# Fewer idle products at the start, x tiles 0 and 1 on ScalarE's queue, wv ahead of x tiles 4 to 7, and another order behind 72 fixed operations: an adaLN block on one Trainium2 core

## The chip, the core and the metric

The kernel runs on one core of a Trainium2 chip. The metric is the device time of one execution in microseconds, the median over several runs. A core has TensorE (PE in the profile; its weight loads have a row of their own, PEld), VectorE (DVE), ScalarE (ACT), GpSimd (POOL) and SyncE (SP), and 16 DMA engines that all queues share. Each engine takes its instructions strictly in the order of its own list, so an instruction that waits holds up all behind it.

## What is computed

The input x has 2048 rows of 512 values, in bfloat16. Cut to what matters:

```python
mod = (silu(c) @ w_mod).reshape(1, 6, 1, 512)
sa, ca, ga, sb, cb, gb = mod[:, 0], ..., mod[:, 5]
h = layernorm(x) * (1 + ca) + sa
x = x + ga * A(h)       # attention: 32 heads of 16; row s sees rows s, s-2, ..., s-14; then @ wo
h = layernorm(x) * (1 + cb) + sb
x = x + gb * B(h)       # (silu(h @ w1) * (h @ w3)) @ w2, hidden width 1792
```

c is one row of 512 values, w_mod is 512 x 3072, wqkv is 512 x 1536, wo 512 x 512, w1 and w3 512 x 1792, w2 1792 x 512.

## The kernel before, in words

The rows of x are 16 tiles T of 128 rows. Nothing is ordered by loops: `_build` makes a list of 1197 operations (`Program.op`), each with its engine, a function that emits its instructions, and the values that it reads and writes. Two long lists written into the file, `ORDER` and `SLOTS`, then say in which order the operations are put onto their engines and which buffer (or PSUM bank) each value takes. `Program.place` deals `ORDER` out to the five engines' lists, and `Program.synchronize` adds a semaphore wait wherever an operation needs another engine's result or a buffer that is still in use. So `ORDER` fixes each engine's instruction list, SyncE's DMA list among them; a DMA is issued by SyncE unless it is built with another `eng`. The costs given to the operations (among them `WMOD`, `PACKET` and `MM`) are of use only to the search that made the lists; no instruction depends on them.

The steps that the text below speaks of, with the profile's line numbers:

- *The modulation.* c is loaded by a DMA of ScalarE's queue, goes through a tanh (L456, after a load of ScalarE's function table) and two VectorE operations (L458, L460), is turned into columns by a TensorE transpose (L462) and copied to `csz` (L464). The first third of w_mod (shift and scale of the first layer norm) comes in four pieces `wms0_0` to `wms0_3` of 256 KB, one DMA each. `modulation(0)` multiplies each piece as it comes (L480, 32 products of 8 columns in all, eight to a piece), and L491 copies the result to `modc`.
- *Idle products.* `warm(n)` puts n products of `ones` with `ones` on TensorE (L502, 512 columns each), whose result nobody reads. `WARMS` says how many stand ahead of the first, second, third and fourth piece, and how many after the last.
- *The first layer norm.* Per tile VectorE takes the statistics (L542, L543), GpSimd the power -0.5 (L547, L549), VectorE normalizes (L554), TensorE transposes (L614), and ScalarE (L622) or VectorE (L629) evict with shift and scale into `h`, which needs `modc`. Tiles are grouped `LN1` = [0, 1], [2, 3], [4..7], [8..11], [12..15]; the last group is transposed by DMA.
- *Projections.* q and k by L666 with evictions at L674 and L675, v by L685 with eviction at L695 and a store to a scratch in DRAM. Group [0, 1] is multiplied piece by piece as the four parts of `h` are there; the other groups wait for the whole of `h`.
- *Attention*, for two tiles at a time: VectorE multiplies q with eight shifted k (L716), TensorE sums over each head (L725, 32 small tiled products), a softmax runs on VectorE and ScalarE, 4 DMAs per tile fetch shifted v from the scratch (`vsh`), VectorE weighs them (L800), TensorE sums (L809, 8 tiled products in four column strips), ScalarE evicts (L815), a DMA transposes, TensorE multiplies with wo (L833) and VectorE adds to x (L837).
- *The gated feed-forward*, for the groups `FFN`: w1 and w3 products (L849, 256 or 512 columns), then w2 products (L892, and L880 for the last two tiles), and the sum with x (L908) goes out. w1, w3 and w2 come in four column groups each, so a product on columns `fi` needs the group's DMA alone (`w1_0` holds the column blocks fi 0 to 3, and so on).

All loads but c are DMAs of SyncE. Its list begins x0, x1, the four pieces, wk, x2 and x3, wq, x4 to x7, wv, x8 to x11, x12 to x15.

Of the kernel before, what the change touches and what calls it, by code (L numbers as in the profile page):

```python
# [267 lines left out]
WMOD = 120  # L268
WARMS = (8, 3, 3, 4, 2)
# [9 lines left out]
def _build(p, A_x, A_wqkv, A_wo, B_w1, B_w3, B_w2, c, w_mod, out):  # L279
# [4 lines left out]
    x_view = x2d.rearrange("(t p) d -> p t d", p=P)  # L284
# [4 lines left out]
    x_sb = sb([P, NT, D], bf, "x")  # L289
# [120 lines left out]
    vx = [Val(f"x{T}") for T in range(NT)]  # L410
# [7 lines left out]
    for T in range(2):  # L418
        p.dma(x_sb[:, T, :], x_view[:, T, :], ("load", 1), (128, 1024), w=[vx[T]])
# [580 lines left out]
]  # L1000
SLOTS = [
# [47 lines left out]
```

## Time and profile before

| | |
|---|---|
| median of 3 runs | 242.54 us (242.08, 242.72, 242.54) |
| the profiled execution's own time | 242.59 us |
| its span, first to last instruction | 240.6 us |
| granted TensorE clock in the profile | 1.00 |
| TensorE busy | 232.7 us, 97% of the span |
| VectorE / ScalarE busy | 168.3 us (70%) / 157.9 us (66%) |
| DMA | 38.33 MB, 159 GB/s over the span |
| idle products L502 | 20 in the program, 19 in the records, 534 ns mean |

The profiled execution is 2.0 us longer than its span and 0.05 us over the median. TensorE's busy time counts each product from its start to its modelled end, and products overlap, so a long busy bar does not mean that products start as fast as they can. How fast they start is read from the times between starts: 0.43 us for a product of 512 columns early on, 0.216 us later, and half of that for 256 columns. A few records of products are missing.

### The profile page before, as it was taken

The page shows a single profiled execution, that of the slowest core. Times are in us where ns is not written, and L with a number is a line of the kernel's source. Part 1 is how long each engine was busy: PE and PEld are TensorE (multiplying, and loading weights), DVE is VectorE, ACT ScalarE, POOL GpSimd, SP SyncE. Part 2 cuts the span into 40 slices and gives each one's busy share as a digit, 9 for nine tenths or more (in the row PEclk, how much of TensorE's full clock was granted, in tenths as well). Part 3 has the DMA queues.
Part 4 walks back from the last instruction along what each step waited for, and adds up shares of the span by engine and source line. Part 5 has one row for each costly group of instructions (what it writes and reads, how often), then busy time and mean ns, then how long its engine had stood idle before and what let it go on. Part 6 is the DMA issues. An engine that isn't in the chain of part 4 may idle for free.

```text
span 240.6 us, 4592 instructions
## 1 busy us (share of the span) xinstructions
PE 232.7 (97%) x1794; PEld 136.3 (57%) x1820; DVE 168.3 (70%) x287; ACT 157.9 (66%) x329; POOL 21.1 (9%) x54
## 2 busy tenths in 40 slices
PE   7989999999999999999999999999999999999995
PEld 2557644545577867664444444444474447576774
DVE  4489999999999999999999658335453224152352
ACT  2169687988999888768858988746754583422310
POOL 4254110000001000130000110001000100000000
DMA  6997999699499959696875963454302000301011
GB/s 191 354 321 226 284 227 248 188 289 346 131 243 270 280 163 226 183 315 101 236 184 166 204 196 75 100 152 45 89 15 52 3 0 3 85 24 65 3 44 45
DMA packets 44125, 38.33 MB, mean 159 GB/s; under 512 B 19512, under 2 KB 34888, under 8 KB 44104
## 3 DMA queue, kind: packets, MB, share of 16 engines
q1 hardware_dynamic: 44096, 38.04, 59.5%
q8 instruction: 14, 0.23, 0.4%
q14 instruction: 7, 0.06, 0.1%
q10 hardware_dynamic: 8, 0.00, 0.0%
HBM read 29.62 MB, written 4.21 MB: 141 GB/s over the span
## 4 chain that ended last, share of the span: by engine, by line
PE 79%; DMA 7%; ACT 5%; DVE 3%; SPq 2%; issue 2%; POOL 1%
PE pall L849 32%; PE pall L892 14%; PE pall L666 10%; PE pall L833 5%; PE pall L685 4%; DMA sb_w<-in_B_w_dram 4%; PE pall L809 3%; PE pall L725 3%; PE pall L502 3%; PE pall L880 3%; SPq L124 2%; DMA sb_h<-sb_xn 2%; DMA out_dram<-sb_o 2%; PE pall L614 1%; ACT sb_h L622 1%
## 5 line engine op out<-in xcount | busy, mean ns | idle before, releaser
L849 PE MATMUL pall<-sb_h,sb_w 128*128 128x256 bf16 (+1 forms) x666 | 102.5, 308 | 1.1 <-ACT sb_hh L859 0.4
L849 PEld LDWEIGHTS pall<-sb_h,sb_w 128*128 128x128 bf16 x672 | 64.7, 98 | 37.3 <-ACT sb_hh L859 1.5
L855 ACT ACTIVATE sb_sg<-pall 128x256 bf16<-128x256 f32 (+1 forms) x84 | 36.5, 457 | 33.3 <-PE pall L849 29.4
L892 PE MATMUL pall<-sb_w,sb_hh 128*128 128x512 bf16 x189 | 43.4, 379 | 0.6 <-issue 0.3
L716 DVE TENSOR_TENSOR sb_pq<-sb_q,sb_kT 128x4096 bf16<-128x4096 bf16 x16 | 36.5, 2283 | 0.0
L666 PE MATMUL pall<-sb_h,sb_wqkv 128*128 128x512 bf16 (+1 forms) x156 | 30.9, 336 | 1.1 <-ACT sb_h L622 0.5
L892 PEld LDWEIGHTS pall<-sb_w,sb_hh 128*128 128x128 bf16 x196 | 19.0, 98 | 21.4 <-issue 0.4
L859 ACT ACTIVATE sb_hh<-pall 128x256 bf16<-128x256 f32 (+1 forms) x56 | 26.3, 491 | 6.9 <-PE pall L849 6.7
L800 DVE TENSOR_TENSOR sb_vsh<-sb_vsh,sb_al 128x4096 bf16<-128x4096 bf16 x13 | 29.5, 2285 | 0.4 <-ACT sb_al L784 0.4
L908 DVE TENSOR_TENSOR sb_o<-pall,sb_x 128x512 bf16<-128x512 f32 (+1 forms) x18 | 11.1, 626 | 22.4 <-PE pall L892 14.3
L860 DVE TENSOR_TENSOR sb_hh<-sb_sg,sb_hh 128x256 bf16<-128x256 bf16 (+1 forms) x56 | 18.4, 352 | 11.4 <-ACT sb_hh L859 7.6
L666 PEld LDWEIGHTS pall<-sb_h,sb_wqkv 128*128 128x128 bf16 x160 | 14.6, 98 | 12.7 <-ACT sb_h L622 0.9
L863 DVE TENSOR_TENSOR sb_hh<-sb_sg,pall 128x256 bf16<-128x256 bf16 x28 | 10.9, 416 | 12.8 <-PE pall L849 11.4
L622 ACT ACTIVATE sb_h<-pall,sb_modc 128x256 bf16<-128x256 bf16 (+1 forms) x22 | 13.2, 673 | 8.8 <-DVE sb_modc L491 7.0
L574 POOL TENSOR_SCALAR sb_rs<-sb_var 128x2 f32<-128x2 f32 x8 | 3.5, 434 | 151.4 <-ACT sb_xn L568 151.4
L833 PE MATMUL pall<-sb_wo,sb_ot 128*128 128x512 bf16 x61 | 15.5, 380 | 0.3 <-issue 0.2
L599 ACT ACTIVATE sb_h<-sb_h,sb_modc 128x512 bf16<-128x512 bf16 (+1 forms) x20 | 13.2, 723 | 3.3 <-DMA sb_h<-sb_xn 3.3
L685 PE MATMUL pall<-sb_wqkv,sb_h 128*128 128x512 bf16 x59 | 15.0, 380 | 0.4 <-issue 0.2
L568 ACT ACTIVATE sb_xn<-sb_x,sb_nm 128x512 bf16<-128x512 bf16 x16 | 11.4, 714 | 5.9 <-DVE sb_nm L564 5.9
L579 ACT ACTIVATE sb_xn<-sb_x,sb_nb,sb_rs 128x512 bf16<-128x512 bf16 x16 | 12.7, 810 | 3.4 <-DVE sb_nb L576 3.4
L837 DVE SCALAR_TENSOR_TENSOR sb_x<-pall,sb_x 128x512 bf16<-128x512 f32 x16 | 10.9, 687 | 2.7 <-PE pall L833 2.6
L675 ACT ACTIVATE sb_kT<-pall 128x512 bf16<-128x512 f32 (+1 forms) x20 | 9.8, 519 | 3.5 <-PE pall L666 3.5
(84 smaller groups left out, 222.1 us busy)
## 6 DMA issues: line engine op xcount, KB each, us to landing
sb_vsh<-v_scratch_dram SPq DMA_DIRECT2D x52, 256.0 KB, 4.6
sb_w<-in_B_w_dram SPq DMA_DIRECT2D x6, 512.0 KB, 7.3
sb_vshx<-v_scratch_dram SPq DMA_DIRECT2D x12, 256.0 KB, 4.6
sb_w<-in_B_w_dram SPq DMA_DIRECT2D x6, 384.0 KB, 5.6
v_scratch_dram<-sb_v SPq DMA_DIRECT2D x16, 128.0 KB, 3.9
out_dram<-sb_o SPq DMA_DIRECT2D x14, 128.0 KB, 1.9
sb_wqkv<-in_A_wqkv_dram SPq DMA_DIRECT2D x3, 512.0 KB, 7.0
sb_x<-in_A_x_dram SPq DMA_DIRECT2D x3, 512.0 KB, 8.8
```

The costliest lines, as they stand in the source:

```text
L599: return e.activation(vh.at[:, ft, 0:n * P], vh.at[:, ft, 0:n * P], ACT.Identity, bias=modc[:, 8 * which + ft:8 * which + ft + 1], scale=m ...
L622: return e.activation(vh.at[:, ft, 0:n * P], b[:, j * 512:j * 512 + n * P], ACT.Identity, bias=modc[:, 8 * which + ft:8 * which + ft + 1], ...
L666: ins = e.matmul(bank(vp)[:, 0:n], wqkv[:, t, kind * D + ft * P:kind * D + (ft + 1) * P], vh.at[:, t, 0:n], start=(t == ORDER[0]), stop=(t ...
L685: ins = e.matmul(bank(vp), vh.at[:, t, tt * P:(tt + 1) * P], wqkv[:, t, 2 * D:3 * D], start=(t == ORDER[0]), stop=(t == ORDER[-1]))
L716: return e.tensor_tensor(vp.at[:], in0, in1, ALU.mult)
L800: return e.tensor_tensor(v_w, v_w, a_w, ALU.mult)
L833: ins = e.matmul(bank(vy), vt.at[:, ft, :], wo[:, ft, :], start=(ft == 0), stop=(ft == KT - 1))
L849: ins = e.matmul(bank(vp)[:, 0:n], wt[:, t, fi * P:(fi + 1) * P], vh.at[:, t, 0:n], start=(t == 0), stop=(t == KT - 1))
L855: p.op("act", lambda e: e.activation(vt.at[:, 0:n], bank(vgp)[:, 0:n], ACT.Silu), c_act(n), k, r=[vgp], w=[vt], table="silu")
L859: p.op("act", lambda e: e.activation(vh_.at[:, 0:n], bank(vup)[:, 0:n], ACT.Copy), c_act(n), k, r=[vup], w=[vh_])
L860: p.op("dve", lambda e: e.tensor_tensor(vh_.at[:, 0:n], vt.at[:, 0:n], vh_.at[:, 0:n], ALU.mult), 60 + n * 69 // 128, k, r=[vt], w=[vh_], ...
L892: ins = e.matmul(bank(vz), vhh[fi].at[:, tt * P:(tt + 1) * P], w2[:, fi, :], start=(fi == 0), stop=(fi == NF - 1))
```

## The change

`WARMS` goes from (8, 3, 3, 4, 2) to (8, 2, 1, 1, 1): 13 idle products in place of 20, all removed ones from between the pieces and after the last. x tiles 0 and 1 are issued by ScalarE, behind c and ahead of the tanh. `ORDER` and `SLOTS` are replaced throughout (1190 operations; the numbers above 67 shift, as seven operations are gone). `WMOD`, a cost for the search, goes from 120 to 125. Which 72 operations were held fixed the lists do not say; the entries that stand ahead of the first k products are all of the start described below.

What the new lists say, read out per engine:

- SyncE: the four pieces, wk, x2 and x3, wq, **wv**, x4 to x7, x8 to x11, x12 to x15. Later `wms1` (1 MB) is the 18th of the list (before: the 40th), and w1_0 and w3_0 come 60th and 62nd, behind the transposes of the attention output of tile 2 (before: 57th and 52nd, ahead of them).
- ScalarE: c, x0, x1, tanh, then the evictions of `h`.
- VectorE, at the start: the same as before up to the evictions, then the statistics of tiles 2 and 3 ahead of a memset (`zrow`) that stood before them.
- TensorE, at the start: 8 idle products, the transpose of c (before: after 7), piece 0, 2 idle, piece 1, 1 idle, piece 2, the transposes of tile 0, 1 idle, piece 3, 1 idle, the transposes of tile 1 (before: both tiles' ahead of piece 2), then k of group [0, 1].
- TensorE, whole list: the tiled products L725 and L809 stand in 15 runs between ordinary products (before: 13). Other than the idle ones, the same products are in both lists.

```diff
-WMOD = 120
-WARMS = (8, 3, 3, 4, 2)
+WMOD = 125
+WARMS = (8, 2, 1, 1, 1)
...
     for T in range(2):
-        p.dma(x_sb[:, T, :], x_view[:, T, :], ("load", 1), (128, 1024), w=[vx[T]])
+        p.dma(x_sb[:, T, :], x_view[:, T, :], ("load", 1), (128, 1024), w=[vx[T]], eng="act")
...
 ORDER = [
-    0, 19, 20, 21, 22, 23, 24, 25, 28, 26, 27, 30, 29, 1, 31, 5, 15, 2, 58, 6, 7, 3, 4, 59, 10, 11, 12, 60, 13, 53, 61, 54, 55, 83, 62, 63,
...
+    0, 19, 20, 21, 22, 23, 24, 25, 28, 26, 27, 29, 30, 31, 1, 5, 15, 2, 58, 6, 7, 3, 4, 59, 10, 11, 12, 60, 13, 53, 61, 54, 55, 76, 62, 63,
+    77, 64, 78, 79, 65, 56, 57, 81, 66, 82, 67, 80, 68, 69, 83, 84, 70, 85, 71, 86, 90, 72, 73, 75, 16, 87, 91, 74, 88, 92, 89, 93, 32, 146,
...
```

In these lists 20 and 21 are x0 and x1, 22 to 25 the pieces, 26 x2 and x3, 27 wq, 28 wk, 29 wv, 30 x4 to x7, and 58 onward the idle products.

124 rows, old and new, of tables (ORDER, SLOTS) are left out of this document.

## The prediction

> **What bounds the kernel now.** I read the page's busy rows first.
>
> ```profile
> PE 232.7 (97%) x1794; PEld 136.3 (57%) x1820; DVE 168.3 (70%) x287; ACT 157.9 (66%) x329; POOL 21.1 (9%) x54
> ...
> PE   7989999999999999999999999999999999999995
> ...
> DVE  4489999999999999999999658335453224152352
> ...
> DMA  6997999699499959696875963454302000301011
> ```
>
> TensorE is full from the third slice to the last but one; VectorE is full beside it up to about 130 us, and the DMA engines up to about 18 us. A full bar can hide waits, so I took the starts of the products from the timeline, TensorE alone. The places where a start comes over 0.3 us later than the product before it explains:
>
> ```profile
> 10.42 3.16 PE L666 MATMUL pall<-sb_h,sb_wqkv 128*128 128x256 bf16 x26 [0.26 <-DVE sb_h L629]
> ...
> 13.92 0.29 PE L614 MATMUL pall<-sb_ident,sb_xn 128*128 128x128 bf16 x2 [0.34 <-DVE sb_xn L554]
> ...
> 16.94 0.61 PE L666 MATMUL pall<-sb_h,sb_wqkv 128*128 128x256 bf16 x4 [0.45 <-ACT sb_h L622]
> ...
> 78.70 1.91 PE L849 MATMUL pall<-sb_h,sb_w 128*128 128x256 bf16 x16 [0.16 <-DMA sb_w<-in_B_w_dram]
> ```
>
> Behind 10.42 they are 0.5 us (13.92), 0.6 (16.94), 0.3 (78.70), and by the same reading 0.6 at 173.09 and 0.3 at 212.64; besides, about 0.16 us after each run of tiled products (L725, L809). So the time is the start up to 10.42, then a sum of products that the change leaves as it is, some 2.3 us of waits, the runs' ends, and 2.5 us behind the last product at 238.1. What the start is made of stands in the chain of waits, in order of time (start, length, what):
>
> ```profile
> 1.50 3.17 PE pall L502 x7
> 4.67 0.11 PE pall L462
> ...
> 5.65 1.30 PE pall L502 x3
> ...
> 7.15 0.87 PE pall L502 x3
> ...
> 8.47 0.18 PE pall L480 x8
> 8.65 0.24 PE pall L502
> ...
> 8.94 0.59 PE pall L502 x2
> 9.53 0.20 PE pall L480 x8
> ...
> 9.95 0.73 DVE sb_h L629 x2
> ...
> 43.73 0.16 issue
> ```
>
> Piece 3 (9.53) follows idle products without a wait. By the tile view of `sb_wm_s`, one issue at a time, the pieces are issued at 1.70, 2.17, 2.65 and 3.12 and land about 3.4, 3.6, 3.8 and 4.7 later, at 5.1, 5.8, 6.5 and 7.8. Each lies there before its turn (5.44, 6.96, 8.47, 9.53): the idle products, not the DMAs, set when the modulation ends. wk, issued at 3.60, lands at 9.4, ahead of 10.42.
>
> **The change part by part.** *Idle products.* Between the pieces stand 1.30 + 0.87 + 0.83 us of them, the last term from 8.65 to 9.53 without the issue row. Two, one and one stay, 0.43 us each while products run slowly, 0.22 after. The clock steps up inside the product that starts at 7.01.
>
> *x0 and x1 on ScalarE.* It delays the chain of c:
>
> ```profile
> 0.79 0.87 SPq L124 DMA_DIRECT2D sb_x<-in_A_x_dram  x2
> ...
> 1.36 1.28 ACT L456 ACT_TABLE_LOAD   x1 [1.36 <-PEq L1034]
> ...
> 3.42 0.67 DVE L542 BATCH_NORM_STATS2 sb_st<-sb_x 128x6 f32<-128x512 bf16 x1
> ...
> 4.83 0.18 DVE L464 COPY sb_csz<-pall 128x4 bf16<-128x4 bf16 x1 [0.52 <-PE pall L462]
> ```
>
> Two issues now stand between c and the table load. They took 0.39 and 0.41 us on SyncE, with gaps about 0.9, so table load, tanh and the two operations on c end 0.9 us later, at 4.4 for 3.5. TensorE does not feel that: eight idle products last to 5.1. VectorE does: the statistics of tile 0 stand behind the operations on c and ahead of the copy to `csz`, so they run 4.4 to 5.3 (0.9 us with L543) and the copy moves from 4.83 to 5.27, 0.44 later. x0 itself takes 2.1 us to land alone, so 3.4; with half the engines' share (0.37 us of data doubled) 3.8, still ahead of 4.4. On SyncE everything moves up by 0.9 us: the pieces land between 0 and 0.9 earlier, and do not bind.
>
> Piece 0's products end at 5.65 + 0.44 = 6.1. Two idle products (0.87) 7.0, piece 1 (0.19) 7.15, one idle (0.43) 7.6, piece 2 7.8, four transposes of tile 0 (half of the 0.45 that eight took) 8.0, one idle (0.22) 8.2, piece 3 8.4, against 9.73: 1.3 us earlier. But tile 1's transposes now come last: one idle product and 0.23 bring them to 8.9 if the clock is up, 9.5 if not. Evictions start at 9.0 (9.5), before at 9.95. **Gain 0.95 us, or 0.45 at the other end**; I take 0.95, since the step at 7.01 lies before these products. k starts 0.47 after the evictions as before, at 9.5, behind wk at 9.4 or earlier. What is late next: wq, landed at 11.6 before, 0 to 0.9 earlier now; k needs 1.7 us from 9.5, so q asks at 11.2. Covered, or 0.4 lost.
>
> *The two waits after it.* The one at 13.92 goes back to the statistics of tiles 2 and 3 (from 10.87, behind the evictions and `zrow`, 0.26). They now begin at 9.8 and `zrow` follows them, so x2 and x3 (landed at 10.1, earlier by up to 0.9 now) bind instead, and the transposes are due about 0.9 us earlier, as k is. ScalarE's four evictions behind the wait at 16.94 keep their lengths; between tile 2's transposes and the next product on that `h` stand eight v products (1.7 us) in the new list. Of 1.1 us I let 0.2 go; bounds 0.5 gained, 0.3 lost.
>
> *wv ahead of x4 to x7.* Issued at 5.91 and 5.14, they landed at 14.6 and 13.1. Swapped, wv comes 1.5 us earlier, in time for v from about 13.5, where it would otherwise make TensorE wait up to 1.1. x tiles 4 to 7 come 1.5 later, 13.7 to 14.6; their statistics started at 14.17. VectorE loses 0 to 0.45; their transposes stood at 18.2 and later, so TensorE does not see it. Without that cover it costs 0.45.
>
> *The order behind the start.* Two more runs of tiled products: 2 x 0.16 = **0.3 us lost** (bounds 0 and 0.5, the latter with the 0.26 us that a run ending on L809 costs at 86.54). The wait on w3_3 at 78.70 should go: 20.5 us of products, by their steps, stand between L809 of tile 2 and the first product on w3_3. A new one is close: w1_0 is now issued behind the transposes of tile 2's output. From that L809 (before at 61.7) to the evicted copy went 1.26 us, the transpose's issue is 1.25, and the weight issue after it (65.33) landed 4.5 us on: 7.1. In the new list, between the two stand one L809 set (0.43), k (0.86), eight half-width w1 and w3 sets (8 x 0.43), two L833 sets (1.73), L725 (0.5) and one transpose set (0.22): 7.2 us. So a wait of 0 to 2, the latter with the 6.5 us that the next weight took (67.03 to 73.55). I take 0.3, the same as the wait that goes; at 4.5 us the DMA queue was as empty as it will be there.
>
> *The end.* In both lists the last product is the second half of one of the last two tiles' column halves: nothing.
>
> Sum: -0.95 - 0.2 + 0.3 + 0.3 - 0.3 = **-0.85 us; 242.59 - 0.85 = 241.7**, 0.05 less against the median. About 0.3%, 0.73 us, is what a measurement can tell here, so this is just beyond it.
>
> **The rivals.** *Cold array (slower).* Products ran at 0.43 us from 1.50 until inside the one at 7.01, with TensorE hardly idle. Now it has nothing from 5.2 to 5.7 and fewer products after. If what steps the rate up counts from 5.7, and needs the same 5.9 us, it comes at 11.6: evictions at 9.5 (0.5 lost) and 2.1 us of k and q products at half rate (1.05 lost): 243.3. It decides once the step comes later than about 9. For it: before, nothing idle stood ahead of the step, and now half a microsecond does. Against: gaps of 0.5 and 0.6 us later in the trace are followed by full-rate products. [...]
>
> *Weights late (slower).* w1_0 and w3_0 land as late as the third weight of that stretch before: 6.5 us rather than 4.5 and more behind `vsh` loads: 2.0 us of wait at about 69 to 72 in place of 0.3, 243.4. For it: 7.1 against 7.2 us leaves nothing. Against: little is queued ahead.
>
> *The start does not arrive.* Pieces earlier, but wq or tiles 2 and 3 hold the products, and the later order costs its 0.3: 242.6.
>
> *A fuller order.* The waits at 78.70, 173.09 and 212.64 (1.2 us) go and none comes: 240.7.
>
> **How the numbers follow.** Forecast 0.45 (own range 241.2 to 242.3, two thirds of it below 241.81); fuller order 0.18, faster; start not arriving 0.10, same; cold array 0.13, of which 0.08 is beyond 243.27; weights late 0.14, of which 0.12 is. Faster 0.30 + 0.18 = 0.48; slower 0.20; same 0.32. The range 240.6 to 243.6 takes in all five.
>
> **What would show it.** Right: piece 3's products end near 8.4, k starts near 9.5, products take 0.11 us (256 columns) from there; `csz` is copied near 5.3; the same waits of about 0.5 us before 17; 15 tiled runs; a short wait on `sb_w` near 69. Wrong: k products 0.21 us apart (cold array); a wait over 1 us on `sb_w` between 63 and 75; a `csz` copy before 5; or new waits of TensorE on VectorE's attention products (L716, L800), of which the trace before has none over 0.3 us.

## The result, and the profile after

The changed kernel is slower: 245.83 us (median of 17 runs, 242.6 to 248.79) for 242.54 (241.73 to 243.83, 17 runs); the ratio is 1.0089, with a 95% interval of 1.006 to 1.0118, about 2.2 us. The ratio leaves out the six runs of after that lie over 1.5% above its fastest, all with a granted clock of 0.979 to 0.993, so it is smaller than the quotient of the medians. The profiled execution took 244.34 us with a span of 242.4, so 1.75 us more than the one of before (242.59, 240.6); all differences between traces below are against that.

The page's busy rows after, the same four as before:

```profile
PE 232.2 (96%) x1786; PEld 136.0 (56%) x1813; DVE 167.8 (69%) x287; ACT 157.7 (65%) x329; POOL 22.8 (9%) x54
...
PE   6899999998998999999999999999999999999995
...
DVE  3687999999897999999999897671142313062352
...
DMA  6997949999689989589898973812300001011011
```

TensorE is busy for 0.5 us less and the span is 1.8 us longer: the loss is waiting. The bar shows where (a slice is 6.06 us): a six and an eight in the first two slices, a seven and a nine before, and eights at 54 to 61 and 73 to 79 us, where before had nines. From the timeline, TensorE alone (start, length, operation, count, idle time before and its releaser), the starts that the product ahead does not explain:

```profile
6.05 0.19 PE L477 MATMUL pall<-sb_mbase,sb_ident 128*128 128x8 bf16 x1 [0.84 <-DVE sb_csz L464]
...
6.32 1.01 PE L502 MATMUL pall<-sb_ones 128*128 128x512 bf16 x2
...
8.40 0.63 PE L502 MATMUL pall<-sb_ones 128*128 128x512 bf16 x1
...
10.68 1.92 PE L666 MATMUL pall<-sb_h,sb_wqkv 128*128 128x256 bf16 x16 [0.58 <-DVE sb_h L629]
12.97 1.65 PE L666 MATMUL pall<-sb_h,sb_wqkv 128*128 128x256 bf16 x13 [0.37 <-ACT sb_kT L675]
...
60.32 1.04 PE L685 MATMUL pall<-sb_wqkv,sb_h 128*128 128x512 bf16 x4 [0.73 <-ACT sb_v L695]
...
72.26 0.60 PE L849 MATMUL pall<-sb_h,sb_w 128*128 128x256 bf16 x4 [0.35 <-ACT sb_sg L855]
...
76.33 1.91 PE L849 MATMUL pall<-sb_h,sb_w 128*128 128x256 bf16 x16 [0.87 <-DMA sb_w<-in_B_w_dram]
```

k starts at 10.68, for 10.42 before and 9.5 forecast. The waits of 0.5 and 0.6 at 13.92 and 16.94 are one of 0.5, at 12.97. New are 0.9 at 60.32, 0.5 at 72.26 and 1.0 at 76.33 (between starts). At 72.26 the releaser named is a ScalarE tile, but `w1_0` landed at 72.12. The wait at 78.70 is gone, and the ones at 173.09 and 212.64 with it.

The chain of waits in order of time (start, length, what) names the start, the weights' stretch and one transfer between them:

```profile
1.38 3.61 DMA sb_x<-in_A_x_dram
5.01 0.70 DVE sb_st L542
...
6.46 0.87 PE pall L502 x2
...
9.47 0.65 PE pall L614 x4
...
51.95 7.69 DMA v_scratch_dram<-sb_v
59.67 0.60 ACT sb_v L695
...
67.92 0.54 SPq L124
68.50 7.69 DMA sb_w<-in_B_w_dram
76.33 1.91 PE pall L849 x16
```

Before, the start's chain was idle products; now its first transfer is x0, 3.6 us from issue to landing, its second a store of v (7.7 us, and ScalarE's evictions one after another behind it), and its third `w3_0`. Adding up by stage what the products start later than the product ahead explains (missing records taken out), and the start up to the first k:

| stage | before | after | difference | forecast |
|---|---|---|---|---|
| first k product | 10.42 | 10.68 | +0.26 | -0.95 |
| from there to 20 us | 1.40 | 0.81 | -0.59 | -0.2 |
| 20 to 60 us | 1.13 | 1.45 | +0.32 | 0 |
| 60 to 80 us | 0.62 | 3.11 | +2.49 | 0 (+0.3 - 0.3) |
| behind 80 us | 3.18 | 2.60 | -0.58 | +0.3 (two more runs' ends, anywhere) |
| sum | | | +1.90 | -0.85 |

The sum agrees with the span's 1.8. Two terms carry the miss: the start (1.2 us) and the stretch of the weights (2.5 us, of which 1.5 are the waits at 72.26 and 76.33 and 0.9 the one at 60.32).

VectorE's timeline at the start shows the first of them:

```profile
5.01 0.69 DVE L542 BATCH_NORM_STATS2 sb_st<-sb_x 128x6 f32<-128x512 bf16 x1 [0.63 <-DMA sb_x<-in_A_x_dram]
...
5.84 0.16 DVE L464 COPY sb_csz<-pall 128x4 bf16<-128x4 bf16 x1
6.54 0.69 DVE L542 BATCH_NORM_STATS2 sb_st<-sb_x 128x6 f32<-128x512 bf16 x1 [0.55 <-DMA sb_x<-in_A_x_dram]
```

VectorE waits for x0 (landed 4.99) and again for x1 (6.52), and the copy that piece 0 needs stands between the two.

### The profile page after: what moved, and what is told of

Read it like the earlier page. It is cut to its first block, busy times and chain, and to the rows that moved or that the text cites. A ratio compares the mean times of both kernels' runs of the same rounds, so it can differ in the third digit from the quotient of the medians.

```text
span 242.4 us, 4585 instructions
## 1 busy us (share of the span) xinstructions
PE 232.2 (96%) x1786; PEld 136.0 (56%) x1813; DVE 167.8 (69%) x287; ACT 157.7 (65%) x329; POOL 22.8 (9%) x54
## 4 chain that ended last, share of the span: by engine, by line
PE 78%; DMA 8%; ACT 4%; DVE 4%; SPq 3%; issue 1%; ACTq 0%; DVEq 0%
PE pall L849 38%; PE pall L892 17%; PE pall L666 6%; PE pall L833 4%; DMA v_scratch_dram<-sb_v 3%; DMA sb_w<-in_B_w_dram 3%; SPq L124 3%; PE pall L809 3%; PE pall L880 3%; PE pall L685 2%; DVE sb_pq L716 2%; PE pall L725 2%; DMA sb_x<-in_A_x_dram 1%; PE pall L614 1%; ACT sb_oa L815 1%
## 5 line engine op out<-in xcount | busy, mean ns | idle before, releaser
L855 ACT ACTIVATE sb_sg<-pall 128x256 bf16<-128x256 f32 (+1 forms) x84 | 35.1, 458 | 33.1 <-PE pall L849 30.7
L860 DVE TENSOR_TENSOR sb_hh<-sb_sg,sb_hh 128x256 bf16<-128x256 bf16 (+1 forms) x56 | 17.6, 349 | 17.6 <-ACT sb_hh L859 13.8
L574 POOL TENSOR_SCALAR sb_rs<-sb_var 128x2 f32<-128x2 f32 x8 | 2.8, 349 | 154.7 <-ACT sb_xn L568 154.7
L685 PE MATMUL pall<-sb_wqkv,sb_h 128*128 128x512 bf16 x60 | 15.1, 380 | 0.9 <-ACT sb_v L695 0.7
L599 ACT ACTIVATE sb_h<-sb_h,sb_modc 128x512 bf16<-128x512 bf16 (+1 forms) x20 | 13.1, 719 | 2.6 <-DMA sb_h<-sb_xn 2.6
L695 ACT ACTIVATE sb_v<-pall 128x512 bf16<-128x512 f32 x16 | 9.6, 607 | 4.8 <-PE pall L685 2.7
```

Of the source, the lines that this page charges most:

```text
L599: return e.activation(vh.at[:, ft, 0:n * P], vh.at[:, ft, 0:n * P], ACT.Identity, bias=modc[:, 8 * which + ft:8 * which + ft + 1], scale=m ...
L685: ins = e.matmul(bank(vp), vh.at[:, t, tt * P:(tt + 1) * P], wqkv[:, t, 2 * D:3 * D], start=(t == ORDER[0]), stop=(t == ORDER[-1]))
L855: p.op("act", lambda e: e.activation(vt.at[:, 0:n], bank(vgp)[:, 0:n], ACT.Silu), c_act(n), k, r=[vgp], w=[vt], table="silu")
L860: p.op("dve", lambda e: e.tensor_tensor(vh_.at[:, 0:n], vt.at[:, 0:n], vh_.at[:, 0:n], ALU.mult), 60 + n * 69 // 128, k, r=[vt], w=[vh_], ...
```

## The experiments

Theory: x0 and x1 cost the start by landing late, and late `w1_0` and `w3_0` cost about 1 to 2 us on their own. Rivals: the few idle products leave a slow array; the new order as a whole is worse; wv ahead of x tiles 4 to 7 costs. Every ratio is against the kernel before, run on the same chip, with its 95% interval.

| kernel | ratio | interval | k starts | waits 60 to 80 us |
|---|---|---|---|---|
| the change | 1.0089 | 1.006 to 1.0118 | 10.68 | 3.11 |
| a_x_sp | 1.0096 | 1.0063 to 1.0129 | 10.47 | 2.43 |
| a_idle20 | 1.0092 | 1.0064 to 1.0121 | 11.98 | 4.03 |
| a_fill | 1.007 | 1.0044 to 1.0097 | 10.73 | 1.30 |
| a_w_early | 1.0051 | 1.0019 to 1.0083 | 11.43 | 1.60 |
| a_x_sp_idle20 | 1.0054 | 1.0021 to 1.0086 | 10.02 | 2.53 |
| b_start | 1.0071 | 1.0045 to 1.0097 | 10.94 | 0.19 |
| b_x_act | 1.0072 | 1.0045 to 1.0098 | 12.01 | 0.30 |
| b_idle13 | 0.9996 | 0.9976 to 1.0017 | 10.66 | 0.43 |
| b_wv | 1.0031 | 1.0008 to 1.0053 | 10.35 | 0.44 |
| best1 | 0.9967 | 0.9948 to 0.9987 | 9.48 | 0.64 |
| best1_x_act | 1.0033 | 1.0006 to 1.0061 | 11.29 | 1.04 |
| best1_late_w | 1.0063 | 1.004 to 1.0086 | 9.62 | 3.64 |

The last two columns are of one profiled execution each (before: 10.42 and 0.62); that of a_idle20 took 246.72 us, 1.3 more than its median.

**Parts of the start, in the kernel before.** b_start makes both edits of the start, b_x_act moves x0 and x1 only, b_idle13 takes idle products away only; the order behind is that of before.

```diff
 # b_x_act and b_start
-        p.dma(x_sb[:, T, :], x_view[:, T, :], ("load", 1), (128, 1024), w=[vx[T]])
+        p.dma(x_sb[:, T, :], x_view[:, T, :], ("load", 1), (128, 1024), w=[vx[T]], eng="act")
 # b_idle13 and b_start
-WARMS = (8, 3, 3, 4, 2)
+WARMS = (8, 2, 1, 1, 1)
```

b_start: 

> The kernel before, in its own order, with two edits of the start: 13 idle products (8, 2, 1, 1, 1) and x tiles 0 and 1 on ScalarE's queue. Cold-array and late-x theories (the start alone costs the time): slower than before by 1 to 4 us, with a scatter over 3 us as the changed kernel has. Order theory (the new order loses the time behind the start): within 0.7 us of before or faster.

b_x_act: 

> The kernel before with x tiles 0 and 1 on ScalarE's queue as its only edit; 20 idle products, its own order. In that order the transposes of both tiles stand ahead of piece 2. Late-x theory: x1 lands at about 6.5 us, is normalized at about 9, so piece 2, piece 3 and k come later: k at 11.2 to 12 instead of 10.4, 0.8 to 1.5 us slower than before. Cold-array theory alone: the idle products are all there, so 0 to 0.5 us, and no execution in which the full rate is taken back.

b_idle13: 

> The kernel before with 13 idle products (8, 2, 1, 1, 1) as its only edit; x on SyncE, its own order. Weight-bound theory (k cannot start before wk has landed, 9.2 to 10.3 us in the traces so far): the modulation ends at about 8.5, k starts at 9.4 to 10.4, so the gain is 0 to 1 us where the clock stays. Cold-array theory: in a good part of the executions the full rate comes late or is taken back for one or two windows of 3.4 us (a granted clock of 0.986 or 0.993), and the median is 0 to 1.5 us slower than before. If neither holds: faster by 1 us or more.

Moving x0 and x1 alone costs 0.72%, 1.7 us, a little more than expected and as much as both edits together; k starts 1.6 us later. A slow array has no part in it: the idle products of b_x_act are 0.2 us apart from 6.14 on, and then TensorE waits for tile 1, whose x landed at 6.85 (TensorE's timeline):

```profile
9.54 0.51 PE L614 MATMUL pall<-sb_ident,sb_xn 128*128 128x128 bf16 x6 [1.11 <-DVE sb_xn L554]
```

Both theories of the start expected a scatter over 3 us. b_start's six runs lie within 0.9 us of each other, so they don't show the 6 us that lie between the fastest and the slowest run of the changed kernel. Taking idle products away alone changes nothing that can be told. In b_idle13's trace the modulation's last products start at 8.32 instead of 9.37, but k waits 2.0 us for wk, which landed at 10.52 in that execution (9.37 in the trace of before). The idle products stood in time that wk mostly covers.

**Undoing parts of the change.** a_x_sp puts x0 and x1 back on SyncE, a_idle20 puts the 20 idle products back, a_x_sp_idle20 does both, and a_fill puts two more ahead of piece 0, where TensorE has nothing.

```diff
 # a_x_sp, a_x_sp_idle20: eng="act" removed from x0 and x1
-WARMS = (8, 2, 1, 1, 1)
+WARMS = (8, 3, 3, 4, 2)     # a_idle20, a_x_sp_idle20
+WARMS = (10, 2, 1, 1, 1)    # a_fill
```

a_x_sp: 

> The changed kernel with x tiles 0 and 1 issued by SyncE again, ahead of the pieces; all else as changed. Late-x theory (x0 landed at 4.99 us instead of 2.90 because its packets share the engines with the pieces, and with it the copy to csz, piece 0 and the normalization of tile 1): x0 lands at 2.9, csz is copied at 5.2 to 5.3, k starts at about 9.3 to 9.5 instead of 10.7, the median falls by 1.2 us or more against the changed kernel. Cold-array theory (the idle products that are left let the step to the full rate come late, or be taken back, in many executions): the gap ahead of piece 0 shrinks from 0.8 to 0.2 us, so the step comes earlier in some executions; median falls by 1 to 3, the scatter stays over 3 us since the products are still 13. Late-weights theory (w1_0 and w3_0): nothing of the waits near 72 and 76 changes, 0.

a_idle20: 

> The changed kernel with the 20 idle products (8, 3, 3, 4, 2) of before, the seven put back behind those that stand in the same place; x still on ScalarE, the new order otherwise. Cold-array theory: the scatter falls to that of before (about 2 us between fastest and slowest), the median falls by 1 to 3 us against the changed kernel although 7 products (1.5 us at full rate) are added ahead of k. Late-x and late-weights theories: the start only gets longer, k at 11.5 to 12.5 and the median 1 to 1.5 us higher.

a_fill: 

> The changed kernel with two more idle products ahead of the transpose of c (10, 2, 1, 1, 1), 0.86 us of work that lies in the 0.84 us in which TensorE waits for the copy to csz. Cold-array theory, idle gap as its cause: the full rate is no longer taken back (9 of 17 executions of the changed kernel show it), the median falls by 0.5 to 1.5 us against the changed kernel, k moves by less than 0.3. Cold-array theory, few products behind it as the cause: share of such executions as before. Late-x and late-weights theories: no difference.

a_x_sp_idle20: 

> The change with both of its edits of the start undone: x tiles 0 and 1 on SyncE and 20 idle products, tile 1's transposes still behind the last of them. What is left of the change is its order, wv ahead of x tiles 4 to 7 and the late weights. If the start costs +1.5 us and the rest of the order +0.7: k at 10.3 to 10.9, ratio 1.001 to 1.005. If the loss lies in the order behind the start: 1.007 or more. If it lies in the start alone and the rest gains: 0.996 to 0.999.

a_x_sp gained nothing, against the theory. Its TensorE timeline says where the early x went:

```profile
8.54 0.39 PE L614 MATMUL pall<-sb_ident,sb_xn 128*128 128x128 bf16 x4
10.47 1.91 PE L666 MATMUL pall<-sb_h,sb_wqkv 128*128 128x256 bf16 x16 [1.54 <-DMA sb_wqkv<-in_A_wqkv_dram]
```

Tile 1's transposes come 0.9 us earlier than in the change, and then TensorE waits 1.5 us for wk, landed at 10.34 in that execution. In a_x_sp_idle20 wk landed at 9.04, k started at 10.02, and the loss that is left, 0.54%, lies behind the start: waits of 0.7 and 1.2 on the weights. Its ratio lies just above the range of the first expectation (a dear start and 0.7 us more) and below that of the second (the loss behind the start); the trace decides for the second, since the start is 0.4 us earlier than before. a_idle20 gained nothing, but it can't decide alone, since its seven products themselves delay k (11.98). a_fill speaks against the slow array as the main cause: the full rate was granted from 4.41 on, and k still starts at 10.73, because x1 landed at 7.07 and tile 1 is normalized behind it (VectorE's timeline):

```profile
7.09 0.69 DVE L542 BATCH_NORM_STATS2 sb_st<-sb_x 128x6 f32<-128x512 bf16 x1 [1.40 <-DMA sb_x<-in_A_x_dram]
```

Two of a_fill's 12 executions had a clock share below 0.995, for 9 of 17 of the change: this fits the expectation that filling the gap keeps the rate. The middle of a_fill's interval is 0.2% below that of the change, but the intervals overlap.

**The weights.** a_w_early issues `w1_0` and `w3_0` ahead of both attention transposes and leaves the rest of the change.

```diff
 SyncE's list, by the names of its entries
-w3_1, v store, w1_2, w1_3, w2_1, ot tile 3, vsh, ot tile 2, w1_0, vsh, w3_0
+w3_1, v store, w1_2, w1_3, w2_1, w1_0, w3_0, ot tile 3, vsh, ot tile 2, vsh
```

> The changed kernel with the DMAs of w1_0 and w3_0 issued ahead of the transposes of the attention output of tile 3, where w2_1 is just done, instead of behind those of tile 2. Late-weights theory: the TensorE gaps at 72.3 (0.5 us) and 76.3 (1.0 us) go, the median falls by 1.0 to 1.5 us against the changed kernel, scatter unchanged. The other theories: 0 within 0.5 us, the gaps go but something else is late by the same amount, or the time is lost elsewhere.

The waits on `sb_w` go and the stretch keeps 1.60 us of waits for 3.11. Two of them are new, 0.6 and 0.3 on the transposes now queued behind the weights (TensorE's timeline):

```profile
68.53 1.04 PE L833 MATMUL pall<-sb_wo,sb_ot 128*128 128x512 bf16 x4 [0.47 <-DMA sb_ot<-sb_oa]
```

The ratio falls from 1.0089 to 1.0051, 0.9 us, with overlapping intervals.

**A kernel composed from this, and two of its parts put back.** best1 keeps the new order behind the start and wv ahead, with x0 and x1 on SyncE, 18 idle products, tile 1's transposes as soon as tile 1 is normalized (ahead of piece 3), and `w1_0`, `w3_0` ahead of `w2_1`, while `w1_3` takes `w1_0`'s late place.

```diff
-WARMS = (8, 2, 1, 1, 1)
+WARMS = (8, 3, 2, 2, 3)
 # x0, x1: eng="act" removed
 TensorE's list
-piece 2, transposes of tile 0, idle, piece 3, idle, transposes of tile 1, k
+piece 2, transposes of tile 0, transposes of tile 1, 2 idle, piece 3, 3 idle, k
 SyncE's list
-w1_2, w1_3, w2_1, ot tile 3, vsh, ot tile 2, w1_0, vsh, w3_0
+w1_2, w1_0, w3_0, w2_1, ot tile 3, vsh, ot tile 2, w1_3, vsh
```

best1: 

> The new order with four edits: x tiles 0 and 1 on SyncE; 18 idle products (8, 3, 2, 2, 3); the transposes of tile 1 ahead of piece 3; w1_0 and w3_0 issued ahead of w2_1, and w1_3 where w1_0 stood. If the three causes (late x, cold array, late weights) are all there is, the start is that of before (k at 10.4 to 10.8, full rate throughout) and the waits between 60 and 80 us fall from 3.1 to under 1 us, while the order behind 80 us keeps its 1.2 us fewer waits: 1 to 1.5 us faster than before. If the order has a loss of its own that the traces don't show: the same as before or slower.

best1_x_act: 

> The composed kernel with one thing put back: x tiles 0 and 1 on ScalarE's queue. Theory (the two x tiles cost the start by landing 2 to 3 us later, whatever stands around them): the copy to csz comes at 5.5 to 5.9 instead of 4.89, tile 1 is normalized near 9 and k starts at 10.6 to 11 instead of 9.48: 1.2 to 1.7 us slower than the composed kernel, ratio to the kernel before 1.002 to 1.004. Rival (the x tiles cost only where few idle products leave a cold array): the clock is up before 7 us as in the composed kernel, k starts before 9.9, ratio 0.997 to 0.999.

best1_late_w: 

> The composed kernel with one thing put back: w1_0 and w3_0 as late in SyncE's list as in the change, behind the transposes of tile 2's attention output. Theory (the late weights cost TensorE about a microsecond by themselves): waits on sb_w between 63 and 77 us that sum to 1.0 to 1.8 us, 0.9 to 1.5 us slower than the composed kernel, ratio to the kernel before 1.000 to 1.003. Rival (the start's delay is what made them late, so that they are hidden with a good start): waits there below 0.4 us, ratio 0.996 to 0.998.

best1 beats both kernels, by less than the 1 to 1.5 us expected: 241.79 us (240.88 to 242.35) for 242.4 of before on that chip, 0.8 us by the ratio. VectorE's timeline of best1, and behind it that of best1_x_act, which differs in the queue of x0 and x1 alone:

```profile
3.42 0.67 DVE L542 BATCH_NORM_STATS2 sb_st<-sb_x 128x6 f32<-128x512 bf16 x1
...
4.89 0.17 DVE L464 COPY sb_csz<-pall 128x4 bf16<-128x4 bf16 x1 [0.57 <-PE pall L462]
4.97 0.68 DVE L542 BATCH_NORM_STATS2 sb_st<-sb_x 128x6 f32<-128x512 bf16 x1
```

```profile
5.31 0.69 DVE L542 BATCH_NORM_STATS2 sb_st<-sb_x 128x6 f32<-128x512 bf16 x1 [0.93 <-DMA sb_x<-in_A_x_dram]
...
6.14 0.16 DVE L464 COPY sb_csz<-pall 128x4 bf16<-128x4 bf16 x1
6.82 0.69 DVE L542 BATCH_NORM_STATS2 sb_st<-sb_x 128x6 f32<-128x512 bf16 x1 [0.53 <-DMA sb_x<-in_A_x_dram]
```

Everything stands 1.25 to 1.9 us later, and both statistics wait for a DMA where none did. The copy and k (9.48 to 11.29) come a little later than expected, and the ratio lies within the expectation of the theory. It is 0.66%, 1.6 us, above that of best1: the size found in the kernel before. But this is not x alone: the full rate was granted from 9.59 on in best1_x_act's trace and from 4.26 on in best1's, so a slow array has a part in k's delay, and the rival's condition (the clock up before 7 us) was not met. The pair that has x alone is b_x_act and the kernel before. For best1_late_w, TensorE's timeline:

```profile
71.51 0.60 PE L849 MATMUL pall<-sb_h,sb_w 128*128 128x256 bf16 x4 [0.75 <-DMA sb_w<-in_B_w_dram]
...
76.75 1.91 PE L849 MATMUL pall<-sb_h,sb_w 128*128 128x256 bf16 x16 [2.03 <-DMA sb_w<-in_B_w_dram]
```

The start is as good as in best1, and the waits on the two weights come to 3.1 us between starts: more than expected (1.0 to 1.8), and the ratio, 0.96% or 2.3 us above that of best1, is outside the expectation too. The four corners, with the change itself as the fourth (there 13 idle products and tile 1's transposes last, in the others 18 and tile 1's transposes ahead of piece 3; `w1_3` takes the place that the two weights leave):

| | `w1_0`, `w3_0` early | late |
|---|---|---|
| x0, x1 on SyncE | 0.9967 | 1.0063 |
| x0, x1 on ScalarE | 1.0033 | 1.0089 |

By the middles of the intervals each costs less when the other is there too, by 0.4% (1.0 us). The four intervals together leave about 0.5% to either side of that, so the times alone don't show it. The traces fit it: `w3_0` lands at 76.6 with the early start and at 76.2 with the late one, so a late start would use up part of the wait for it. In a_x_sp both stood against a gain: k came only 0.2 us earlier in its trace, for wk, and from 60 to 80 us it still waits 2.4.

**wv ahead.** b_wv does this alone in the kernel before.

```diff
-x2 and x3, wq, x4 to x7, wv, x8 to x11
+x2 and x3, wq, wv, x4 to x7, x8 to x11
```

> The kernel before with one thing done: wv issued ahead of x tiles 4 to 7. By the prediction's step this costs nothing to TensorE (bounds: 0.45 us lost by the statistics of tiles 4 to 7, up to 0.5 gained where v waits for wv): wv lands near 13.1 for 14.6, x tiles 4 to 7 near 14.6 for 13.1, ratio 0.998 to 1.001. Rival: VectorE, full from 10 to 130 us, hands the later statistics on to the attention products, ratio 1.002 or more.

It costs 0.31%, 0.75 us. x tiles 4 to 7 landed at 15.1 (before 13.1), and TensorE's timeline has a wait that before had not:

```profile
20.19 0.29 PE L614 MATMUL pall<-sb_ident,sb_xn 128*128 128x128 bf16 x2 [0.66 <-DVE sb_xn L554]
```

In the trace of the change no wait of that kind stands: with x tiles 4 to 7 landed at 14.5, the first of these transposes starts at 20.53 there, at 18.25 before. So the move is dear in the old order; what it brings in the new one was not run alone.

## Why the prediction was wrong, point by point

- *x0 and x1 on ScalarE: the step that failed first.* The prediction had x0 landing at 3.4 to 3.8 and the copy to `csz` at 5.27, and it let x1 go without a price. Measured: x0 at 4.99, x1 at 6.52 (2.90 and 3.38 before), the copy at 5.84. The condition stated for an error was a copy before 5; it erred the other way. Issued 0.6 us later and on another queue, the two tiles shared the engines with the pieces: piece 0 to 3 landed at 3.61, 4.76, 6.00 and 7.35 instead of 5.14, 5.81, 6.48 and 7.79, with x1 between pieces 2 and 3. The chain of c was indeed 0.9 us later (table load at 2.25 for 1.36), and was not what bound.
- *Piece 3's end at 8.4, k at 9.5.* Measured 9.25 and 10.68. Of the 0.85 us up to piece 3's end, 0.35 is the late copy (piece 0's products end at 6.45, not 6.1) and 0.5 the slow products: idle products take 0.43 us up to k. The other 0.3 up to k are tile 1's transposes, which end at 10.1 and not at 8.9. With x back on SyncE (a_x_sp) the copy comes at 5.25, piece 3's products end at 8.3, these transposes at 8.9, and the evictions start at 9.04, all within 0.1 of the forecast; then k waits for wk. So the sum of the start was right but for x, with some luck: the copy waits there for TensorE and not for tile 0. best1's k at 9.48 meets the forecast too, but with more idle products, and wk, landed at 9.35, sets it.
- *"k starts behind wk at 9.4 or earlier".* True in the changed kernel (9.21), but wk came at 10.34 and 10.52 in a_x_sp and b_idle13, and then it was the bound. The rival "the start does not arrive" named wq or tiles 2 and 3; the one that can hold it is wk.
- *Cold array.* Its mechanism was there: the record of the granted clock has full rate from 10.25 on, later than the rival's point of decision, 9. But the k products of the profiled execution are 0.11 us apart, and b_x_act and a_fill say that it is not what bounds the start. In 9 of the 17 runs of after the clock's share was below 0.995; their median was 246.84, that of the other eight 244.45. In b_idle13 four of 12 runs had such a share (median 243.15, the other eight 242.1). In b_start five of six had it, and they took no longer (243.96 to 244.88) than the sixth (244.85). So a lowered share goes with longer executions in some kernels; how much longer it makes them was not separated.
- *The two waits after the start.* 0.6 us gained for 0.2 forecast: bounds right, size low.
- *Weights late: the term that was mis-sized most.* Forecast 0.3 us, with 4.5 us from issue to landing for `w1_0`. `w1_0` took 4.8, which made a wait of 0.5; but the prediction priced only that one, and `w3_0`, two places behind it, took 7.7 us and made another of 1.0: 1.5 us of waits for 0.3. The rival had 2.0 us at about 69 to 72 and its reason, a landing as slow as the third weight's 6.5 us; the argument against it, "little is queued ahead", looked at the wrong side: by the landing times it is the `vsh` loads issued between and behind the two (67.92 to 73.12, landed 73.05 to 81.05) that are in flight with them. That these make `w3_0` late was not tested by a run. In best1_late_w the price was 3.1 us of waits.
- *The wait at 78.70.* It did go, but the prediction read it wrongly: `w3_3` had landed at 73.55, and the transfer that landed just ahead of 78.70 was `w1_3` (issued at 68.86, landed at 78.56). The new list issues `w1_3` at 54.28.
- *A wait that was not thought of.* At 60.32 the v products wait 0.9 us for ScalarE's eviction of v, which the chain traces to a v store issued at 51.95 and landed 7.7 us later. Behind it ScalarE works without a pause up to the evictions that the transposes ahead of `w1_0` need, so this store has a part in how late the weights are issued. Its size changes from trace to trace: ahead of the same products TensorE is idle for 0.2 to 1.0 us in four others of the new order, and in the remaining four the view shows no idle time there. No run moved the store alone.
- *wv ahead at nothing.* In the old order it cost 0.75 us; the cover named (transposes late enough) was not there at 20.19.
- *The order behind 80 us.* Forecast 0.3 lost, measured 0.6 gained; the waits at 173.09 and 212.64 went as the rival "fuller order" had it. What the order is worth by itself was not run: best1's 0.33% (0.8 us) comes with a k that starts 0.94 us earlier than in the kernel before. From the first k product to the end of the span, the traces of before, best1 and best1_x_act take 230.2, 229.4 and 229.7 us, those of a_w_early and the change 230.2 and 231.7.

The forecast's sign failed on two places, x and the weights. By the middles of the corners x costs about 1.6 us and the weights 2.3, the two together 3.0; the composed kernel gains 0.8 without them, which leaves the 2.2 us measured.

## What to carry to other kernels

A transfer moved to another queue was here not only issued at another time: it shared the engines with what it had stood ahead of, and x0 took 3.6 us from issue to landing instead of 2.1. So price the landing of every moved transfer from rows where as much is in flight, down to the last one moved, and follow its reader: VectorE's copy to `csz` stood behind the statistics of x0 and started at 5.84, with its input there at 5.22. When a group of weights is moved back in the queue, price the last of the group, with what is issued between and behind it: `w3_0` took 7.7 us where `w1_0` took 4.8. Work on a critical path that is taken away can be covered by a load that lands just as late, as wk did in b_idle13 (k at 10.66 for 10.42). And two delays at different places may hide each other: undoing x alone gained nothing here (a_x_sp), undoing x and the weights did (best1), so take them out together before calling either harmless.

## What the runs showed of the hardware

- *On one queue x landed first, on two it shared.* x0 took 2.1 to 2.2 us from issue to landing when issued first on SyncE's queue, and 3.3 (a_fill) to 4.4 (a_w_early) on ScalarE's, beside the pieces. The four pieces and two x tiles together were there at 7.79 before and 7.35 after: the order changed much more than the rate (334 and 336 GB/s from 4 to 7 us). Both queues moved packets side by side: in the three half microseconds from 3.5 to 5.0 of the changed kernel's trace 64, 74 and 71 of SyncE's and 58, 80 and 62 of ScalarE's. x1, issued at 1.77, landed at 6.52, between pieces 2 (6.00) and 3 (7.35), which were issued on the other queue at 1.7 and 2.2.
- *In b_start the full rate was taken back after 3.4 us that were 65% busy.* In its trace the idle products and pieces between 4.3 and 7.7 us ran at full rate, and the next 6.8 us at half; in five of the six runs the clock's share was 0.986. The windows view (window, length, busy time and count of each engine, the granted clock of TensorE, DMA share, GB/s):

```profile
4.30:7.70 3.40, 2.21 (x25) 1.01 (x24) 2.19 (x7) 0.00 (x0) 1.51 (x4) 1.00 1.05 357
7.70:14.50 6.80, 5.66 (x41) 3.82 (x42) 3.66 (x11) 1.76 (x4) 2.12 (x6) 0.50 1.10 350
14.50:20.00 5.50, 5.04 (x44) 3.54 (x42) 5.50 (x18) 3.66 (x10) 2.43 (x6) 1.00 0.78 220
```

  TensorE was busy for 2.21 us of the 3.40 and lost the rate; in the next 6.8 us, busy for 5.66, it ran at half, and behind them at the full rate again. These two records of the clock last 3.41 and 6.83 us. What decides stays open, and the busy time of 3.41 us alone doesn't: counted in such stretches from where the record has the full rate begin, b_idle13 lost it after one with 1.53 us of work (6.61 to 10.02), but a_x_sp kept it through one with 2.14 (6.40 to 9.82) and a_fill through one with 1.69 (7.82 to 11.23). best1, busy for 2.75 of 3.41 us from 4.26 on, kept it in that trace, and its share was 1.00 in all of 12 runs.
- *Landing times scatter.* wk, issued at 3.6 with the same six transfers ahead of it on SyncE, landed at 9.04, 9.35, 9.37, 9.40, 9.88, 10.34 and 10.52 in the seven traces of that order. Why was not found. The two latest are a_x_sp and b_idle13, the two of the seven with 13 idle products; whether that is chance, one trace of each can't tell.
